# Rotating the start of the gated values inside their tiles

## The chip, the core and the metric

The kernel runs on one core of one Trainium2 chip. The metric is the time of the program on the device in microseconds (us). The program is run several times, and the median counts.

## What is computed

For each batch and head a matrix state of 48 x 48 complex numbers is carried along 768 time steps, decayed by a complex factor and fed with an outer product; its real part is read with q. The result, as a 3072 x 384 matrix, goes through a gated feed-forward block.

```python
batch, n_heads, seq, head_dim = 4, 8, 768, 48          # d_model 384, d_ff 1536
for t in range(S):
    S_re, S_im = ar * S_re - ai * S_im + kv, ar * S_im + ai * S_re
    y[:, :, t] = einsum('bhd,bhde->bhe', q[:, :, t], S_re)
...
g = x @ w_gate
silu = g * (1.0 / (1.0 + np.exp(-g)))
val = x @ w_val
return (silu * val @ w_out).astype(np.float32)
```

## The kernel before

The 3072 tokens are cut into 24 slabs of 128 tokens (four batches times six pieces of 128 steps), and two slabs make a group, so there are 12 groups. The attention part of a group is prepared by VectorE, ScalarE and small matmuls (`stage_ops`, `slab_ops`) and ends in the transposed activations of the group, 256 tokens wide, as a rounded high part `xh` and the rest `xl`. Then the feed-forward part of the group runs (`ffn_ops`), in 12 chunks of 128 of the 1536 inner columns.

For chunk f of group g (g from 1 on; group 0 runs in plain float32 with other tiles) the steps are these. `f1` (line 886) makes the gate and the value of the chunk in one PSUM bank: 18 matmuls, each with its own weight load of 128 x 128 from the weight tiles `ww`, with 256 columns of `xh` or `xl` streaming. ScalarE applies silu into `sg` (line 896), and VectorE multiplies by the value (line 901). The product is split: `hh` is a cast of `sg` to the float32r type (lines 332 on ScalarE or 334 on VectorE, by `cast`), and `hl` is the difference `sg - hh` (line 328, by `tt`). `f2` (line 925) multiplies back: six matmuls, where `hh` or `hl` is the stationary operand (a weight load of 128 x 128 each) and 384 columns of the output weights `wo` stream; for each half of the tokens the order is `hh` with the high weights, `hh` with the low weights, `hl` with the high weights. Twelve chunks accumulate in two PSUM banks, which are then copied to `ost` and stored.

`hh` and `hl` have two buffers each (`slots`), so chunk n waits for what chunk n - 2 left. The order of all instructions on all engines is computed beforehand by a planner that simulates the engines with given costs (`Planner.plan`); f2 of a chunk stands behind f1 of the next chunk or the one after it. The attention work of later groups is put between the chunks of earlier ones.

Tiles are made by `new`. Pools give addresses in the order in which names are first made, and some small tiles stand only to move what follows. In the kernel before, taken modulo 512 bytes, `wo` and the stage tiles begin at 320, `ww` at 384 (tiles 0 to 6 and 9 to 11) or 128 (7, 8 and -1), the values inside `xh` and `xl` at 320 or 64 (`begin` is 48 elements, 192 bytes, into tiles at 128 or 384), the triangular mask at 384, and all buffers of `hh` and `hl` at 128. Slices of a tile that line 886 or 925 uses lie whole multiples of 512 bytes apart. So in f1 and f2 from group 1 on, the stationary operand begins 64 or 320 bytes after the moving one, modulo 512. `hh` and `hl` are the last tiles in the memory.

Of the kernel before, what the change touches and what calls it, by code (L numbers as in the profile page):

```python
# [20 lines left out]
P = 128  # L21
# [4 lines left out]
NF = DF // P  # L26
# [173 lines left out]
def quick(ctx, tc, q, k, v, a_re, a_im, w_in, w_out, out, count):  # L200
# [4 lines left out]
    work = ctx.enter_context(tc.tile_pool(name="work", bufs=1))  # L205
# [66 lines left out]
    for t in STAGES:  # L272
        SHAPE[t] = ([P, 2 * H, D], F32)
    slots = dict(qs=1, ks=1, T=2, dec=3, sc=2, sg=2, hh=2, hl=2, ost=2, xh=2, xl=2, vt=2,
                 gv=2, po=1, ps=2, py=1, pm=1)
# [6 lines left out]
    for t, (nm, f, i) in {"re": ("w", 0, 0), "im": ("w", 0, 1), "s1": ("o", 0, 0), "s2": ("w", 1, 0), "s3": ("w", 1, 1),  # L282
                          "qt": ("o", 1, 0), "kt": ("o", 2, 0), "qs": ("w", 2, 0)}.items():
        n, nm_f = 96 if t == "qs" else D, (nm, NF - 3 + f)
# [12 lines left out]
    def new(tag, inst):  # L297
        if tag in fixed:
            t = fixed[tag][0]
        elif tag[0] in ("ww", "wo", "bt"):  # L300
            t = None
        elif tag == "ps":
            t = banks[int(inst[-1])]
        elif tag in PSUMS:
            t = psum.tile([P, 512], F32, name="p_" + tag, tag=tag, bufs=2 if tag == "po" else slots[tag])
        else:
            shape, dt = SHAPE[tag]
            if isinstance(inst, tuple) and inst[0] in SPLIT:
                dt = F32R
            if tag == "xh" and inst == 0:  # L310
                dt = F32
            if tag == "xl" and isinstance(inst, str):
                dt = U32
            if tag in SHIFTED:
                n = shape[-1] * (shape[1] if len(shape) > 2 else 1)
                begin = 48 if tag[0] == "x" else 0
                t = work.tile([P, n + (64 if begin else 0)], dt, name=tag, tag=tag, bufs=slots[tag])[:, begin:begin + n]
                if len(shape) > 2:
                    t = t.rearrange("p (k t) -> p k t", k=KT)
            elif tag == "dec":  # L320
                t = work.tile([96, 8 * H], dt, name=tag, tag=tag, bufs=slots[tag])[:, 0:4 * H]
            else:
                t = work.tile(shape, dt, name=tag, tag=tag, bufs=slots[tag])
        at_[tag, inst] = t
        return t
# [26 lines left out]
    def stage_ops(g, first, many):  # L352
# [19 lines left out]
        def load(t, x):  # L372
            def fn(e):
                b0 = 2 * bp + first
                nc.sync.dma_start(out=new(*tg(t)).rearrange("p (b h) d -> p b (h d)", b=many), in_=x[b0:b0 + many, :, c * P:c * P + P, :].rearrange("b h t d -> t b (h d)"))  # L375
            pl.add(f"ld_{t}{N}", {"SP": 0.5}, fn, deps=[held.get(t, "")], alloc=[tg(t)], lat=1.4 if N == "0a" and t in ("re", "im") else LAND if exact else LAND + SPARE, move=0.65 * many)

        def act(name, dst, source, func, table, deps, scale=1.0, bias=None, new_=False):
            def fn(e):
                if new_:  # L380
                    new(*tg(dst))
                kw = {} if bias is None else {"bias": bias}
                nc.scalar.activation(out=of(dst), in_=of(source), func=func, scale=scale, **kw)  # L383
            length = cost(("ACT",), span)
            if bias is not None:
                length["ACT"] += 0.1
            pl.add(name + N, length, fn, deps=[d if "." in d else d + N for d in deps] + [held.get(name, "")], alloc=[tg(dst)] if new_ else [],
                   use=[tg(source)] + ([] if new_ else [tg(dst)]), table=table)
# [4 lines left out]
        if divided:  # L393
            def rec(e):
                nc.vector.reciprocal(out=new(*tg("s3")), in_=of("re"))
            pl.add("rec" + N, {"DVE": 2.5 * span / HD}, rec, deps=["ld_re" + N], alloc=[tg("s3")], use=[tg("re")])
        else:
            act("lnr", "s3", "re", AF.Ln, "ln", ["ld_re"], new_=True)
# [815 lines left out]
```

## Time and profile before

| | us |
|---|---|
| median of 3 runs | 611.21 |
| lowest and highest of them | 610.23, 611.64 |
| span of the profiled execution, first to last instruction | 609.42 |
| TensorE multiplying (PE) | 591.6 |
| TensorE loading weights (PEld) | 562.3 |
| VectorE (DVE) busy | 473.0 |
| ScalarE (ACT) busy | 442.3 |
| GpSimd (POOL) busy | 39.3 |

The time of the profiled execution is given only as its span. The weight load of the next matmul runs beside the matmul before it, so PE and PEld overlap. A matmul's busy time reaches beyond the start of the next one, since they are pipelined; the pace of TensorE is read from start to start.

### The profile page before, as it was taken

The numbers are of one execution on the slowest core, as the hardware profiler recorded it, in microseconds if no ns is written. First come the engines' busy times: TensorE is split into PE (matmuls) and PEld (weight loads), VectorE is DVE, ScalarE is ACT, GpSimd is POOL, SyncE is SP. The second block draws the span as 40 slices with busy tenths as digits, with TensorE's granted clock in tenths as the row PEclk, the third lists the DMA queues.
The fourth block names the chain that finished last, engine by engine and source line by source line (L and its number), as shares of the span: only waits on it lengthen the run. The fifth ranks groups of instructions, "written<-read, shape, count | busy, mean of one in ns | idle before, by whom it ended". The sixth has DMA issues, their size and how long they took to land.

```text
span 609.4 us, 18043 instructions
## 1 busy us (share of the span) xinstructions
PE 591.6 (97%) x7516; PEld 562.3 (92%) x7516; DVE 473.0 (78%) x848; ACT 442.3 (73%) x718; POOL 39.3 (6%) x70
## 2 busy tenths in 40 slices
PE   8789999999999999999999999999999999999996
PEld 7577768999999999999999999999999999999996
DVE  8999999889799778678678678678878867553443
ACT  7999898676976977976985994995996896212221
POOL 4210001010010010010010001001000000000000
PEclk9999999999999999999999999999999999999999
DMA  9999114554554465455545445545644642632220
GB/s 278 359 361 348 23 55 112 130 145 106 150 152 102 123 154 130 122 144 134 129 116 149 122 109 148 131 114 125 157 117 116 172 115 65 147 78 58 79 53 31
DMA packets 132263, 83.15 MB, mean 136 GB/s; under 512 B 106416, under 2 KB 123824, under 8 KB 132176
## 3 DMA queue, kind: packets, MB, share of 16 engines
q1 hardware_dynamic: 129344, 77.09, 46.6%
q0 software_dynamic: 2256, 4.06, 2.9%
q8 instruction: 61, 1.00, 0.7%
q10 hardware_dynamic: 576, 0.79, 0.4%
q14 instruction: 26, 0.21, 0.1%
HBM read 61.40 MB, written 4.78 MB: 109 GB/s over the span
## 4 chain that ended last, share of the span: by engine, by line
PE 84%; DVE 4%; DMA 4%; SPq 3%; ACT 3%; issue 2%
PE p_gv L886 46%; PE p_po L925 24%; PE p_py L707 6%; PE p_ps L664 4%; PE p_pm L478 2%; PE p_pm L713 2%; DMA wo<-in_w_out_dram 1%; SPq L785 1%; SPq L375 1%; DMA ww<-in_w_in_dram 1%; DVE ww L328 1%; DMA qt<-in_q_dram 1%; ACT L1031 1%; ACT xl L332 0%; ACT s L383 0%
## 5 line engine op out<-in xcount | busy, mean ns | idle before, releaser
L886 PE MATMUL p_gv<-xh,ww 128*128 128x256 f32 x1596 | 304.0, 288 | 0.0
L886 PEld LDWEIGHTS p_gv<-xh,ww 128*128 128x128 f32 x1596 | 256.0, 189 | 7.3 <-issue 1.4
L886 PE MATMUL p_gv<-xl,ww 128*128 128x256 f32 x726 | 200.9, 277 | 0.7 <-issue 0.7
L1031 ACT ACT_TABLE_LOAD x124 | 159.1, 1283 | 2.3
L886 PEld LDWEIGHTS p_gv<-xl,ww 128*128 128x128 f32 x726 | 136.4, 188 | 0.2 <-issue 0.2
L925 PE MATMUL p_po<-wo,hh 128*128 128x384 f32 x484 | 124.0, 337 | 0.0
L901 DVE TENSOR_TENSOR sg<-sg,p_gv 128x256 f32<-128x256 f32 x144 | 59.0, 411 | 70.4 <-ACT sg L896 67.2
L896 ACT ACTIVATE sg<-p_gv 128x256 f32<-128x256 f32 x144 | 54.3, 383 | 75.1 <-PE p_gv L886 74.5
L925 PEld LDWEIGHTS p_po<-wo,hh 128*128 128x128 f32 x484 | 81.6, 188 | 0.9 <-issue 0.2
L925 PE MATMUL p_po<-wo,hl 128*128 128x384 f32 x242 | 81.0, 336 | 0.0
L328 DVE TENSOR_TENSOR hl<-sg,hh 128x256 fp32r<-128x256 f32 x132 | 54.7, 421 | 8.0 <-ACT hh L332 2.3
L332 ACT CAST hh<-sg 128x256 fp32r<-128x256 f32 x74 | 30.1, 407 | 30.2 <-DVE sg L901 25.1
L925 PEld LDWEIGHTS p_po<-wo,hl 128*128 128x128 f32 x242 | 45.4, 188 | 0.0
L383 ACT ACTIVATE s<-s 128x768 f32<-128x768 f32 x44 | 37.2, 845 | 10.9 <-DVE s L328 9.2
L707 PE MATMUL p_py<-sc,vt 128*32 128x128 f32 x768 | 37.3, 272 | 2.4 <-ACT ww-1_529 L332 2.4
L664 PEld LDWEIGHTS p_ps<-T 96*32 96x32 f32 x1536 | 28.9, 111 | 4.8 <-issue 3.4
L707 PE MATMUL p_py<-T,G 96*32 96x128 f32 x640 | 33.2, 274 | 0.0
L678 DVE TENSOR_TENSOR sc<-p_ps,tri 128x512 f32<-128x512 f32 x48 | 31.1, 678 | 2.2 <-PE p_py L707 2.2
L664 PE MATMUL p_ps<-T 96*32 96x128 f32 (+3 forms) x1536 | 32.2, 235 | 0.0
L328 DVE TENSOR_TENSOR ks<-kt,s 128x768 f32<-128x768 f32 x22 | 20.9, 952 | 8.3 <-PE p_pm L713 6.7
L707 PEld LDWEIGHTS p_py<-sc,vt 128*32 128x32 f32 x768 | 23.3, 110 | 3.4 <-issue 3.0
L328 DVE TENSOR_TENSOR qs<-qt,s 128x768 f32<-128x768 f32 x22 | 20.8, 950 | 5.1 <-ACT s L383 5.1
(147 smaller groups left out, 839.6 us busy)
## 6 DMA issues: line engine op xcount, KB each, us to landing
T<-turned SPq DMA_DIRECT2D x240, 64.0 KB, 2.1
wo<-in_w_in_dram SPq DMA_DIRECT2D x24, 384.0 KB, 3.6
ww<-in_w_in_dram SPq DMA_DIRECT2D x12, 767.8 KB, 10.5
vt<-in_v_dram SPq DMA_DIRECT2D x24, 288.0 KB, 4.0
wo<-in_w_out_dram SPq DMA_DIRECT2D x12, 384.0 KB, 3.2
wo<-in_w_out_dram SPq DMA_DIRECT2D x12, 383.8 KB, 10.9
re<-in_a_re_dram SPq DMA_DIRECT2D x11, 384.0 KB, 3.8
im<-in_a_im_dram SPq DMA_DIRECT2D x11, 384.0 KB, 4.5
```

What stands on the lines that cost most here:

```text
L328: V[e].tensor_tensor(out=out, in0=a, in1=b, op=op)
L332: nc.scalar.copy(out=out, in_=in_)
L383: nc.scalar.activation(out=of(dst), in_=of(source), func=func, scale=scale, **kw)
L478: nc.tensor.matmul(out=ps, lhsT=tri, rhs=flat(half(x, i)), start=j == 0, stop=j == 1)
L664: nc.tensor.matmul(out=ps[32 * slot:32 * slot + 32, at, 32 * j:P], lhsT=kT[:, h // 2, h % 2, j, :], rhs=qT[:, h // 2, h % 2, j:4, :], star ...
L678: nc.vector.tensor_tensor(out=s.rearrange("p (x h) t -> p x h t", x=2), in0=at_["ps", f"{n}.{qd}"].rearrange("p (x h t) -> p x h t", x=2, ...
L707: nc.tensor.matmul(out=o, lhsT=l, rhs=r, start=opens, stop=closes, tile_position=(0, 32 * slot))
L886: nc.tensor.matmul(out=gv[:, i, :], lhsT=l, rhs=r, start=(m == 0), stop=(m == len(mm) - 1))
L896: nc.scalar.activation(out=new("sg", I), in_=at_["gv", I][:, 0:2 * P], func=AF.Silu)
L901: nc.vector.tensor_tensor(out=sg, in0=sg, in1=at_["gv", I][:, 2 * P:4 * P], op=ALU.mult)
L925: nc.tensor.matmul(out=po, lhsT=l[:, cs], rhs=weight("o", f, part), start=f == 0 and j == 0, stop=f == NF - 1 and j == len(products) - 1)
L1031: nc.scalar.preload_act_table_set(op.load)
```

## The change

In `new`, the values of `hh` and `hl` no longer begin where their buffer begins. Their instance is named "g.f", and from it a start of 4 * (11 * (12 * (g - 1) + f) % 32) elements of four bytes is computed: a multiple of 16 bytes from 0 to 496. Each buffer has 128 elements (512 bytes) more room. `xh` and `xl` keep their start of 48 elements. The same view is written by the cast and the subtraction and read by line 328 and by the weight loads of line 925.

```diff
             if tag in SHIFTED:
                 n = shape[-1] * (shape[1] if len(shape) > 2 else 1)
-                begin = 48 if tag[0] == "x" else 0
-                t = work.tile([P, n + (64 if begin else 0)], dt, name=tag, tag=tag, bufs=slots[tag])[:, begin:begin + n]
+                if tag[0] == "x":
+                    begin, room = 48, 64
+                else:
+                    g, f = map(int, inst.split("."))
+                    begin, room = 4 * (11 * (NF * (g - 1) + f) % 32), 128
+                t = work.tile([P, n + room], dt, name=tag, tag=tag, bufs=slots[tag])[:, begin:begin + n]
```

## Rows read from the trace of the kernel before

**Rows 1.** Page, part 1: busy us (share of the span) x instructions, by engine.

```profile
PE 591.6 (97%) x7516; PEld 562.3 (92%) x7516; DVE 473.0 (78%) x848; ACT 442.3 (73%) x718; POOL 39.3 (6%) x70
```

**Rows 2.** Page, part 4: the chain that ended last, by line.

```profile
PE p_gv L886 46%; PE p_po L925 24%; PE p_py L707 6%; PE p_ps L664 4%; PE p_pm L478 2%; PE p_pm L713 2%; DMA wo<-in_w_out_dram 1%; SPq L785 1%; SPq L375 1%; DMA ww<-in_w_in_dram 1%; DVE ww L328 1%; DMA qt<-in_q_dram 1%; ACT L1031 1%; ACT xl L332 0%; ACT s L383 0%
```

**Rows 3.** By windows: length, busy PE, PEld, DVE, ACT, POOL, granted clock, DMA, GB/s.

```profile
324.00:353.20 29.20, 28.51 (x362) 27.93 (x361) 22.09 (x39) 23.62 (x37) 0.58 (x1) 1.00 0.50 130
353.20:602.00 248.80, 247.69 (x3136) 242.92 (x3130) 167.81 (x327) 150.60 (x271) 6.75 (x11) 1.00 0.43 108
```

**Rows 4.** Timeline of PE, one regular chunk: start us, busy us, instruction, xcount merged.

```profile
585.10 0.51 PE L925 MATMUL p_po<-wo,hh 128*128 128x384 f32 x2
585.44 0.34 PE L925 MATMUL p_po<-wo,hl 128*128 128x384 f32 x1
...
586.13 0.28 PE L886 MATMUL p_gv<-xh,ww 128*128 128x256 f32 x1
...
588.18 0.51 PE L925 MATMUL p_po<-wo,hh 128*128 128x384 f32 x2
```

**Rows 5.** Timeline of PE from 332.5 to 349.2: f2 starts, and one f1.

```profile
332.79 0.52 PE L925 MATMUL p_po<-wo,hh 128*128 128x384 f32 x2
...
339.15 0.52 PE L925 MATMUL p_po<-wo,hh 128*128 128x384 f32 x2
...
340.21 0.28 PE L886 MATMUL p_gv<-xh,ww 128*128 128x256 f32 x1
...
342.33 0.52 PE L925 MATMUL p_po<-wo-1_589,hh 128*128 128x384 f32 x2
...
348.69 0.52 PE L925 MATMUL p_po<-wo,hh 128*128 128x384 f32 x2
```

**Rows 6.** Timeline of PE at 325.2: an f1 matmul after a stop.

```profile
325.20 0.28 PE L886 MATMUL p_gv<-xl,ww 128*128 128x256 f32 x1 [0.69 <-issue]
```

**Rows 7.** Tile `hh`: operation xcount, ns min/median/max, first and last start, shapes.

```profile
L925 PEld LDWEIGHTS p_po<-wo,hh x484: 186/188/192, 110.8 to 603.2; 128*128 128x128 f32 x162
...
L328 DVE TENSOR_TENSOR hl<-sg,hh x132: 407/420/428, 106.8 to 602.6; 128x256 fp32r<-128x256 f32 x132
L332 ACT CAST hh<-sg x74: 386/407/419, 114.9 to 589.3; 128x256 fp32r<-128x256 f32 x74
L334 DVE CAST hh<-sg x58: 278/294/297, 105.8 to 602.3; 128x256 fp32r<-128x256 f32 x58
```

**Rows 8.** Timeline of all engines from 598.4 to 604.2: the last two chunks.

```profile
598.96 0.43 DVE L328 TENSOR_TENSOR hl<-sg,hh 128x256 fp32r<-128x256 f32 x1
...
601.54 0.51 PE L925 MATMUL p_po<-wo,hh 128*128 128x384 f32 x2
...
602.26 0.29 DVE L334 CAST hh<-sg 128x256 fp32r<-128x256 f32 x1
...
602.59 0.42 DVE L328 TENSOR_TENSOR hl<-sg,hh 128x256 fp32r<-128x256 f32 x1
...
602.79 0.96 PE L925 MATMUL p_po<-wo,hh 128*128 128x384 f32 x4
...
603.59 0.51 PE L925 MATMUL p_po<-wo,hl 128*128 128x384 f32 x2
```

**Rows 9.** Page, part 5: groups; xcount | busy us, mean ns of one | idle before.

```profile
L886 PE MATMUL p_gv<-xl,ww 128*128 128x256 f32 x726 | 200.9, 277 | 0.7 <-issue 0.7
...
L925 PE MATMUL p_po<-wo,hh 128*128 128x384 f32 x484 | 124.0, 337 | 0.0
...
L925 PE MATMUL p_po<-wo,hl 128*128 128x384 f32 x242 | 81.0, 336 | 0.0
```

**Rows 10.** Groups by line, the smaller ones: as in the group before.

```profile
L886 PE MATMUL p_gv<-xl,ww-1_529 128*128 128x256 f32 x66 | 18.3, 277 | 0.0
...
L925 PE MATMUL p_po<-wo-1_589,hh 128*128 128x384 f32 x44 | 11.2, 335 | 0.0
...
L925 PE MATMUL p_po<-wo-1_589,hl 128*128 128x384 f32 x22 | 7.4, 336 | 0.0
```

## The prediction

> **What bounds the kernel now.** I read the page's busy times first, then its chain of waits, then the table by windows, then the groups by line, and last the timeline of TensorE, which the argument rests on. TensorE multiplies during 591.6 of 609.4 us, its weight loads cover 562.3, and VectorE and ScalarE stand at 78% and 73% [rows 1]. In the chain that ended last, line 886 (the first matmuls, "f1") has 46% and line 925 (the second, "f2") 24%; no line that writes the gated values `hh` and `hl` is named among the largest [rows 2]. From 353 to 602 us TensorE is busy for 247.7 of 248.8 us, at a granted clock of 1.00, the 2.4 GHz level [rows 3]. So only a change of TensorE's own pace can move the end by much, or a late `hh` or `hl`.
>
> That pace shows in the distance from start to start (the busy time of one matmul overlaps the next one's). In a regular chunk the six f2 matmuls take 586.13 - 585.10 = 1.03 us and the eighteen f1 matmuls 588.18 - 586.13 = 2.05, in all 3.08 [rows 4]. The same instructions run slower in one stretch: f2 340.21 - 339.15 = 1.06, f1 342.33 - 340.21 = 2.12, in all 3.18; six chunks begin 3.18 us apart, from 332.79 to 348.69 [rows 5]. The clock in that stretch is granted at 1.00 as well [rows 3], so this is not the clock. The stretch opens after TensorE had stood still for 0.69 us at 325.20 [rows 6]. I read this as two paces in which the stream of the moving operand and the weight load beside it can settle, about 4 ns a matmul apart, and I call them fast and slow. I count 7 slow chunks: these six and the rest of that stretch.
>
> **The change part by part.** It adds and removes no instruction, wait or DMA, and gives the planner the same costs, so the order stays. It moves where each chunk's `hh` and `hl` begin, in steps of 16 bytes. Per chunk k = 12(g-1)+f the step is 11k mod 32, so that the 132 chunks visit each of 32 starts four or five times.
>
> *The tiles.* Each of the four slots grows by 512 bytes; they lie last, so no other tile moves. 0 us.
>
> *The writes.* Per chunk there is one cast into `hh` (74 on ScalarE of 386 to 419 ns, 58 on VectorE of 278 to 297) and one subtraction into `hl` (407 to 428) [rows 7]. At their fixed starts the spread is 11 to 33 ns. No row shows another start. From above: a VectorE cast could fall to the subtraction's median, 420 - 294 = 126 ns more, 58 x 0.126 = 7.3 us of VectorE's time. From below: nothing gained, since what they finish early waits anyway. Cover: the subtraction that ends at 598.96 + 0.43 = 599.39 serves the f2 at 601.54, 2.1 us later [rows 8]. Without cover stands only the last chunk: its cast at 602.26 releases the f2 at 602.79, while its `hl` (done at 603.01) is wanted at 603.59 [rows 8]. So 0 to 0.13 us; I take 0.
>
> *The weight loads and the f2 matmuls.* These read the moved values: 792 matmuls (484 + 44 on `hh`, 242 + 22 on `hl`) [rows 9, 10], each with its own weight load, which in the groups takes 186 to 192 ns [rows 7] and runs beside the matmul before it. Before the change every such pair stands alike: the weights begin 64 or 320 bytes past the moving operand, modulo 512. That 64 or 320 makes no difference is to be seen: 277 ns for the low values against the common weight tiles, 277 against the one whose start is 256 bytes off (`ww-1`) [rows 9, 10]. What 16, 32 or 128 bytes do, no row shows. The bounds come from the two paces. From above: all chunks slow, (132 - 7) x 0.10 = 12.5 us. From below: the first two matmuls of f2 take 585.44 - 585.10 = 0.34 [rows 4]; six at 0.17 make 1.02 instead of 1.03, 132 x 0.01 = 1.3 us gained; and if nothing but columns counted, 384 at 2.4 GHz are 0.160, six 0.96, a gain of 132 x 0.07 = 9.2 us, as an estimate that no matmul of these rows reaches.
>
> My value lies between: a start 16 bytes on is, to the weight load, the same as reading at another moment beside the stream, and such another moment is what parts slow from fast. With nothing known of 31 of 32 starts, I take half of the chunks as slow in f2: (66 - 7) x 0.03 = 1.8 us. f1 reads nothing that moved, but in the slow stretch the pace was handed from f2 to the f1 behind it and back through six chunks [rows 5]. I take it as handed on in half of these cases, a quarter of all: (33 - 7) x 0.07 = 1.8 us. Sum: 1.8 + 1.8 = 3.6 us. The profiled span of 609.4 becomes 613.0; no time of that execution besides its span is given, and the span lies 1.8 under the median of the three runs, 611.21. So 611.2 + 3.6 = 614.8 us.
>
> One rule speaks against this term. The Trainium skill, "TensorE: Matmul & The Clock Gate", section "Step-by-step: what each phase is for", says that TensorE has two independent read ports, one for the moving operand and one for weights, so that loading the next weights takes nothing from the running matmul. By it the sum is 0 and the time 611.2. The rows agree only in part: by the same page's section "Back-to-back issue gap" 256 columns would take 262 cycles, 109 ns, and f1 takes 2.05 / 18 = 114 in the fast pace and 2.12 / 18 = 118 in the slow one [rows 4, 5].
>
> **The rivals.**
>
> *No start matters (611.2).* The two streams do not touch. For it: 64 and 320 bytes cost the same, and the weight load keeps to 186 to 192 ns through both paces [rows 7, 10]. Against it: something other than work and clock sets two paces, and it has to do with how the two reads stand to each other. The remaining difference is that of runs, 610.2 to 611.6. If it holds, the slow pace is a matter of timing after stops alone, and the starts of `hh` do not choose it.
>
> *Most starts are bad (about 621).* f2 goes slow at nearly every start, and f1 keeps the pace as it did for six chunks: with 107 of 132 slow, (107 - 7) x 0.10 = 10 us, 621. For it: nothing in the stretch from 332.79 to 348.69 brought the pace back [rows 5]. Against it: for most of the run the fast pace returns after each stop, and f1's own pairs stay as they were.
>
> *The other side: faster (609.1).* The present start of `hh` against `wo` is a poor one, and f2's 1.03 is partly lost time; other starts give 0.17 per matmul and a start that changes with every chunk leaves the slow pace no room to last. Then 132 x 0.01 + 7 x 0.10 = 2.0 us are gained. Place: the 792 f2 matmuls and the stretch of [rows 5]. It decides once more than half of the starts run under 1.03 and none tips f1. For it: f2's 0.172 per matmul stands 12 ns above its columns, f1's 0.114 only 7 above its own. Against it: f1's steps scaled from 256 to 384 columns give 0.171 already, so little is left at this level.
>
> **How the numbers follow.** Forecast 0.47, no effect 0.28, most starts bad 0.11, faster 0.14. What can be told from no change is about 0.2%, 1.2 us. The range runs from 609.7, which leaves out most of the faster case (0.09), to 622, which leaves out the far end of the bad case and a third pace that no row shows (0.09). Since cases of both signs are in it: the forecast's own range is 612.2 to 619. Slower by over 0.2%: 0.43 of the forecast, 0.11, and 0.03 of the no-effect case, 0.57. Same: the rest of the forecast, 0.04, most of no effect, 0.22, and 0.02 of faster, 0.28. Faster: 0.12 and 0.03, 0.15.
>
> **What would show it.** Right: f2's six matmuls take between 1.02 and 1.06 us by chunk, and the value repeats with the step (k and k + 32 alike, perhaps k + 16); slow chunks are several times 7, and f1 takes 2.12 behind some slow f2; line 925's matmuls become longer on average, and VectorE's and ScalarE's casts keep their 294 and 407 ns. Wrong: f2 stays at 1.03 for all starts (no effect); f2 moves with the step but f1 never follows, which halves the sum; f2 falls under 1.03 for most steps; or a third pace far above 1.06, which would carry the time over the range. A wait of line 925 for `hh` or `hl` that is longer than before would say that the writes count after all.

## The result and the profile after

The changed kernel takes 615.45 us (615.02 to 615.88, 4 runs) against 611.42 before (610.23 to 612.5, 4 runs). The ratio is 1.0073, with a 95% interval of 1.0052 to 1.0094; here and below the ratio is estimated from the runs with its interval and is not exactly the quotient of the two medians. The forecast was 614.8, slower.

The order of the work is the same; the change's four added lines move line 886 to 890, 925 to 929, 328 to 332, 332 to 336 and 334 to 338. First the busy times and the groups by line of the changed kernel, which answer to [rows 1] and [rows 9].

```profile
PE 595.0 (97%) x7516; PEld 565.9 (92%) x7516; DVE 472.7 (77%) x848; ACT 442.6 (72%) x718; POOL 39.4 (6%) x70
...
L890 PE MATMUL p_gv<-xl,ww 128*128 128x256 f32 x726 | 201.9, 278 | 0.0
...
L929 PE MATMUL p_po<-wo,hh 128*128 128x384 f32 x484 | 125.2, 340 | 0.0
...
L929 PE MATMUL p_po<-wo,hl 128*128 128x384 f32 x242 | 81.4, 337 | 0.0
```

TensorE multiplies for 3.4 us longer, while VectorE and ScalarE stay within 0.3. The f2 matmuls on `hh` went from 337 to 340 ns. f1, which reads nothing that moved, is longer too. Next the tile `hh`, which answers to [rows 7].

```profile
L929 PEld LDWEIGHTS p_po<-wo,hh x484: 186/188/192, 111.2 to 606.8; 128*128 128x128 f32 x162
...
L332 DVE TENSOR_TENSOR hl<-sg,hh x132: 406/420/427, 107.4 to 606.1; 128x256 fp32r<-128x256 f32 x132
L336 ACT CAST hh<-sg x74: 386/407/419, 115.4 to 592.6; 128x256 fp32r<-128x256 f32 x74
L338 DVE CAST hh<-sg x58: 274/294/297, 106.4 to 605.8; 128x256 fp32r<-128x256 f32 x58
```

All medians are those of before: neither the writes nor the recorded weight loads depend on the start. The loss is in the distance from one matmul to the next. The timeline of TensorE over two chunks of the changed kernel, the first of step 16 (256 bytes), the second of step 27:

```profile
545.61 0.51 PE L929 MATMUL p_po<-wo,hh 128*128 128x384 f32 x2
...
546.65 0.28 PE L890 MATMUL p_gv<-xh,ww 128*128 128x256 f32 x1
...
548.69 0.51 PE L929 MATMUL p_po<-wo,hh 128*128 128x384 f32 x2
...
549.75 0.28 PE L890 MATMUL p_gv<-xh,ww 128*128 128x256 f32 x1
...
551.87 0.34 PE L929 MATMUL p_po<-wo,hh 128*128 128x384 f32 x1
```

The first has the fast pace of [rows 4]: f2 1.04, f1 2.04, in all 3.08. The second has that of [rows 5]: 1.06, 2.12, 3.18. Both stand inside a stretch of 247 us at a granted clock of 1.00 (table by windows, columns as in [rows 3]):

```profile
353.00:600.00 247.00, 245.91 (x3153) 241.19 (x3152) 166.82 (x319) 151.44 (x272) 6.75 (x11) 1.00 0.42 109
```

The pace goes with the step. Chunk 49 of the changed kernel (step 27) began its f2 at 299.33:

```profile
299.33 0.51 PE L929 MATMUL p_po<-wo,hh 128*128 128x384 f32 x2
...
300.39 0.28 PE L890 MATMUL p_gv<-xh,ww 128*128 128x256 f32 x1
...
302.51 0.51 PE L929 MATMUL p_po<-wo,hh 128*128 128x384 f32 x2
```

It takes 1.06 and 2.12 like the one at 548.69, chunk 113. Chunk 33 (from 239.73 to 242.91), at step 11 and so 256 bytes away from these, takes 3.18 as well. I took all chunks whose f2 and f1 run without a stop between them and summed the distances from start to start, by step modulo 16 (f is the number of the chunk in its group, 0 to 11):

| step mod 16 | f2, us | f1 behind it, us |
|---|---|---|
| 0 | 1.036 to 1.040; 1.052 in chunk 0 | 2.043 to 2.044; 2.058 in chunk 0 |
| 6, 9, 10, 12 | 1.044 to 1.059 | 2.118 to 2.125 |
| 11 | 1.057 to 1.058; 1.040 for f = 5, behind attention matmuls | 2.119; 2.053 to 2.054 for f = 5 |
| the ten others | 1.039 to 1.064 | 2.044 to 2.063 |

Step 0 alone gives both best values; what precedes the chunk counts too. Since each step of the rotation stands 11 after the one before, a step always follows the same other one, so the table does not part a step's own price from what the chunk before it leaves. Behind 19 of 87 f2 that are followed by an uninterrupted f1, this f1 takes over 2.09; before the change it was 6 of 87. In sums over both traces from the first f2 to the last, the 748 f2 distances without a stop grew from 129.5 to 131.2 us, 1.6 in all. The 2322 f1 distances with their stops grew from 269.1 to 270.4, 1.3: a pace slower by 1.2 ns a matmul, 2.6 us, less 1.3 by which the stops were longer before. Of these 1.3, 0.9 are the stop of [rows 6], which this execution does not have. The remaining 1.0 of the 4.0 us between the spans lies almost all outside these chunks: 0.5 ahead of the first f2, whose first weight load begins at 108.1 instead of 107.6, and 0.4 behind the last f2; no moved value is read there.

### The profile page after: what moved, and what is told of

Same layout as the page of the kernel before. It is cut to its first block, busy times and chain, and to the rows that moved or that the text cites. A ratio compares the mean times of both kernels' runs of the same rounds, so it can differ in the third digit from the quotient of the medians.

```text
span 613.4 us, 18043 instructions
## 1 busy us (share of the span) xinstructions
PE 595.0 (97%) x7516; PEld 565.9 (92%) x7516; DVE 472.7 (77%) x848; ACT 442.6 (72%) x718; POOL 39.4 (6%) x70
## 4 chain that ended last, share of the span: by engine, by line
PE 84%; DVE 5%; DMA 3%; ACT 2%; SPq 2%; issue 2%
PE p_gv L890 46%; PE p_po L929 24%; PE p_py L711 6%; PE p_ps L668 4%; PE p_pm L482 2%; PE p_pm L717 2%; DMA wo<-in_w_out_dram 1%; SPq L789 1%; DVE ww L332 1%; DMA ww<-in_w_in_dram 1%; SPq L379 1%; DMA ww<-in_a_im_dram 1%; ACT L1035 1%; DVE ww L796 1%; ACT xl L336 0%
## 5 line engine op out<-in xcount | busy, mean ns | idle before, releaser
L668 PE MATMUL p_ps<-T 96*32 96x32 f32 (+3 forms) x1536 | 32.2, 235 | 0.0
L890 PE MATMUL p_gv<-xh,ww-1_529 128*128 128x256 f32 x132 | 24.8, 280 | 0.0
```

What stands on the lines that cost most here:

```text
L668: nc.tensor.matmul(out=ps[32 * slot:32 * slot + 32, at, 32 * j:P], lhsT=kT[:, h // 2, h % 2, j, :], rhs=qT[:, h // 2, h % 2, j:4, :], star ...
L890: nc.tensor.matmul(out=gv[:, i, :], lhsT=l, rhs=r, start=(m == 0), stop=(m == len(mm) - 1))
```

## The experiments

All kernels issue the same instructions in the same order. Where a diff shows only a line with `begin, room`, it stands in the place of that line in the change's diff; the others are against the kernel before. In the traces below, line 925 or 929 opens f2 and line 886 or 890 opens f1.

**One fixed start, 160 bytes, for all chunks.**

```diff
-                    begin, room = 4 * (11 * (NF * (g - 1) + f) % 32), 128
+                    begin, room = 40, 128
```

> Every chunk's hh and hl begin 160 bytes into their buffers (step 10); the start no longer changes from chunk to chunk. Theory P (the place of the weight load against the moving operand, modulo 256 bytes, sets each chunk's pace): every chunk is like the chunks of step 10 under the rotation, f2 1.055 and f1 2.12 us instead of 1.036 and 2.044, so 132 x 0.096 = 12.7, less the 0.7 that slow chunks of the kernel before cost already: 623 to 624 us. Rival R (a start that changes redraws the pace, the place itself does not matter): no change from chunk to chunk, so 611.4.

Measured: 615.2 us against 610.9, ratio 1.0061 (1.0038 to 1.0084). Both expectations missed. The start does not change and yet the kernel is slower, so R falls; but the loss is a third of what P gave. The timeline of TensorE, two chunks, f2 and f1 starts:

```profile
288.08 0.52 PE L929 MATMUL p_po<-wo,hh 128*128 128x384 f32 x2
...
289.14 0.28 PE L890 MATMUL p_gv<-xh,ww-1_529 128*128 128x256 f32 x1
...
291.26 0.51 PE L929 MATMUL p_po<-wo,hh 128*128 128x384 f32 x2
...
292.30 0.28 PE L890 MATMUL p_gv<-xh,ww 128*128 128x256 f32 x1
...
294.34 0.34 PE L929 MATMUL p_po<-wo,hh 128*128 128x384 f32 x1
```

Slow and fast chunks take turns: f2 1.06 and f1 2.12, then 1.04 and 2.04. A chunk entered at the fast pace leaves slow, and one entered slow leaves fast. The two buffers of `hh` and `hl` take turns as well, but they do not decide. Chunk 18, counted from 0 over all groups and so an even one, is entered from an f1 of 2.05; it takes 1.05 (from 177.44 to 178.49), and the f1 after it, behind two attention matmuls, 2.12 (178.84 to 180.96). The even chunk 46, at 291.26 above, takes 1.04 and 2.04. So the start and the pace in which the chunk is entered decide together; that second part was missing in P.

**Start at 0 or 256 bytes, changed every second chunk.**

```diff
+                    begin, room = 64 * ((NF * (g - 1) + f) // 2 % 2), 128
```

> The start changes every second chunk between 0 and 256 bytes. Theory P: 256 bytes on is the same place, so 611.4 within 0.2%, f2 1.036 and f1 2.044 in every regular chunk. Rival R: the pace is redrawn at each change of start, half of 132 chunks, so some 2 us and more: 613 to 615. A period of 512 bytes instead of 256: half of the chunks at another pace than 1.036, the time anywhere from 611 to 618.

Measured: 611.5 against 610.9, ratio 1.0011 (0.9994 to 1.0027). The timeline across a change of start:

```profile
577.83 0.51 PE L929 MATMUL p_po<-wo,hh 128*128 128x384 f32 x2
...
580.91 0.51 PE L929 MATMUL p_po<-wo,hh 128*128 128x384 f32 x2
...
583.99 0.51 PE L929 MATMUL p_po<-wo,hh 128*128 128x384 f32 x2
...
587.07 0.33 PE L929 MATMUL p_po<-wo,hh 128*128 128x384 f32 x1
```

The first two chunks begin at 256 bytes, the third, at 583.99, at 0: 3.08 each. A change of start by itself costs nothing, and 256 bytes on is the same place. 128 bytes on is not: step 8 gave 1.044 and 2.057 in the rotated kernel, where step 0, entered from the same f1 time of 2.061, gave 1.036 and 2.044.

**Everything 160 bytes further on.**

```diff
-    const.tile([P, 32], F32, name="before_tri")
+    const.tile([P, 72], F32, name="before_tri")
```

> All tiles of the kernel, hh, hl, wo, ww, xh, xl and the masks, lie 160 bytes further on; every distance between two of them stays as in the kernel before. Theory P (relative place): 611.4. Rival A (the absolute place of the stationary operand decides; hh and hl now begin where step 10 puts them): 623 to 624 as with 160 bytes for hh and hl alone, f2 1.055 and f1 2.12.

Measured: 611.0 against 610.9, ratio 0.9991 (0.9973 to 1.001). The timeline of one chunk:

```profile
568.12 0.51 PE L925 MATMUL p_po<-wo,hh 128*128 128x384 f32 x2
...
569.15 0.28 PE L886 MATMUL p_gv<-xh,ww 128*128 128x256 f32 x1
...
571.20 0.33 PE L925 MATMUL p_po<-wo-1_589,hh 128*128 128x384 f32 x1
```

1.03, 2.05, 3.08, as in [rows 4]. `hh` and `hl` begin at the same offset modulo 512 bytes as in the first experiment, where they were alone in moving. So distances between tiles count, and where the values lie in the memory does not.

**One chunk in twelve at 160 bytes.**

```diff
+                    begin, room = 40 if f == 9 else 0, 128
```

> Only chunk f = 9 of each group begins at 160 bytes, the other eleven at 0. Chunk 9 opens a stretch of about six chunks with nothing but f1 and f2. Theory H (the pace is handed on, as the prediction assumed): f2 of chunk 9 tips the stretch, and chunks 10, 11, 0, 1, 2 stay slow behind it, 11 groups x 6 x 0.096 = 6.3: about 617.5. Theory O (each chunk's own start alone sets its f2 and the f1 behind it): 11 x 0.096 = 1.1: about 612.5.

Measured: 612.3 against 610.9, ratio 1.0016 (1.0002 to 1.0029). By the time H falls, and O's size holds. A usual stretch:

```profile
287.86 0.52 PE L929 MATMUL p_po<-wo,hh 128*128 128x384 f32 x2
...
288.92 0.28 PE L890 MATMUL p_gv<-xh,ww-1_529 128*128 128x256 f32 x1
...
291.04 0.51 PE L929 MATMUL p_po<-wo,hh 128*128 128x384 f32 x2
...
292.07 0.28 PE L890 MATMUL p_gv<-xh,ww 128*128 128x256 f32 x1
...
294.12 0.51 PE L929 MATMUL p_po<-wo,hh 128*128 128x384 f32 x2
```

Chunk 9 costs 3.18, and the next one, at 0 bytes, is back at 3.08. So it goes in nine of the eleven groups. In two another kind of stretch stands, as in [rows 5]:

```profile
383.64 0.51 PE L929 MATMUL p_po<-wo,hh 128*128 128x384 f32 x2
...
386.82 0.52 PE L929 MATMUL p_po<-wo,hh 128*128 128x384 f32 x2
...
390.00 0.52 PE L929 MATMUL p_po<-wo,hh 128*128 128x384 f32 x2
```

Here chunk 10, at 0 bytes, takes 3.18 too, and so do the next two. The displaced chunk 9, at 383.64, did not open this stretch: the f1 ahead of chunk 8 is slow already, 16 matmuls from 375.82 to 377.70, 118 ns each. So at the usual start there are at least two slow settings with the same f1 time. One ends with the next f2. The other goes on through many chunks; here and in [rows 5] it also outlived the attention matmuls between chunks 8 and 9, and it ended with those between chunks 2 and 3 of the next group. A displaced f2 leads into the first; the second is that of the kernel before, and what leads into it was not settled. The trace is of an execution of 616.1 us, 3.8 above the median: its first f2 begins at 110.21, 2.4 us later than in the trace of the kernel before, and the two stretches cost about 1 us.

**Only `hl`, and only `hh`, at 160 bytes.**

```diff
+                    begin, room = 40 if tag == "hl" else 0, 128      # the other run: "hh"
```

> hl alone begins at 160 bytes, hh at 0: 264 of the 792 weight loads stand at another place. Theory L (the load and the matmul beside it lose the time): the loads of hl run beside the second and the fifth matmul of f2, so in a chunk entered at the fast pace these two grow, the others stay: with both tiles at 160 the six were 176, 178, 175, 180, 174, 172 ns instead of 170, 173, 173, 174, 173, 173, so 170, 178, 173, 174, 174, 173, f2 1.042 us and 0.8 us in all at most, f1 2.044: 611.0 to 612. Rival S (any shift of phase in f2 tips the f1 behind it): every second f1 at 2.12 as with both tiles, 66 x 0.077 = 5 us: about 615.

> hh alone begins at 160 bytes, hl at 0: 528 of 792 loads. Theory L: the first, third and fourth matmul of f2 grow (176, 173, 175, 180, 173, 173), f2 1.050, 132 x 0.014 = 1.8 us, and f1 keeps its 2.044 because the last load of hl stands as before: 612.5 to 613. Rival S: every second f1 at 2.12, 5 us more: about 615 to 617.

Measured: `hl` alone 611.2 against 611.7, ratio 1.0000 (0.9984 to 1.0015); `hh` alone 613.7, ratio 1.0046 (1.0026 to 1.0066). A chunk with `hl` moved:

```profile
572.07 0.50 PE L929 MATMUL p_po<-wo-1_589,hh 128*128 128x384 f32 x2
...
573.11 0.28 PE L890 MATMUL p_gv<-xh,ww 128*128 128x256 f32 x1
...
575.15 0.33 PE L929 MATMUL p_po<-wo,hh 128*128 128x384 f32 x1
```

And one with `hh` moved:

```profile
574.20 0.51 PE L929 MATMUL p_po<-wo-1_589,hh 128*128 128x384 f32 x2
...
575.25 0.28 PE L890 MATMUL p_gv<-xh,ww 128*128 128x256 f32 x1
...
577.31 0.51 PE L929 MATMUL p_po<-wo,hh 128*128 128x384 f32 x2
```

With `hl` f2 is 1.04 and f1 2.04; from start to start the six are 170, 172, 177, 176, 175, 173 ns, 1.043. With `hh` f2 is 1.05 and f1 2.06; the six are 176, 173, 180, 174, 172, 178 ns, 1.053. L holds for the sizes of f2 (1.042 and 1.050 expected) and for f1 with `hl`. S falls in both: no f1 takes over 2.09 with `hl`, and 7 of 87 do with `hh`. L misses which matmul pays: with `hl` the third and fourth grow most, where the second and fifth were expected; with `hh` the first, third and sixth, where the first, third and fourth were. And f1 behind a moved `hh` is slower by 0.017, which L did not have; the time of 613.7 is above L's 612.5 to 613 and under S's 615 to 617.

**All chunks at 16 bytes.**

```diff
+                    begin, room = 4, 128
```

> All chunks begin at 16 bytes (step 1), which under the rotation gave f2 1.063 and f1 2.044. If the place alone decides, every regular chunk repeats these: 132 x 0.027 = 3.6 at most, about 614, with f1 at the fast pace throughout. If the pace in which the chunk is entered decides as well, as with 160 bytes where 1.055 and 1.040 took turns, f2 is 1.063 only behind another step, and both numbers change.

Measured: 616.5 against 611.7, ratio 1.0080 (1.0055 to 1.0105). Within the intervals, sixteen bytes in all chunks cost as much as the rotation. The timeline:

```profile
288.32 0.51 PE L929 MATMUL p_po<-wo,hh 128*128 128x384 f32 x2
...
289.37 0.28 PE L890 MATMUL p_gv<-xh,ww-1_529 128*128 128x256 f32 x1
...
291.49 0.51 PE L929 MATMUL p_po<-wo,hh 128*128 128x384 f32 x2
...
292.54 0.28 PE L890 MATMUL p_gv<-xh,ww 128*128 128x256 f32 x1
...
294.59 0.51 PE L929 MATMUL p_po<-wo,hh 128*128 128x384 f32 x2
```

f1 is 2.12 and 2.05 in turns. The same step gave f1 2.044 in the rotated kernel, behind another step. So the second of the two cases expected holds.

**`wo` moved along with `hh` and `hl`.**

```diff
-    work.tile([P, 48], F32, name="ahead", tag="ahead", bufs=1)
+    work.tile([P, 88], F32, name="ahead", tag="ahead", bufs=1)
...
-    work.tile([P, 16], F32, name="behind", tag="behind", bufs=1)
+    work.tile([P, 104], F32, name="behind", tag="behind", bufs=1)
...
+                    begin, room = 40, 128
```

> hh and hl begin at 160 bytes in all chunks, and wo (with the stage tiles that lie behind it) is moved by 160 bytes too, while ww, xh, xl and the mask stay. Against wo, hh and hl stand as in the kernel before; the first load of hh against xh, and that of ww beside the sixth f2 matmul against wo, do not. Theory P: f2's first five matmuls return to 170 to 174 ns; what is lost is at the borders, f2 1.036 to 1.045. Rival (the place against xh, or where hh is written, decides): f2 keeps 1.055 and 1.040 in turns, and f1 2.12 every second time, 615 as with hh and hl alone.

Measured: 615.0 against 611.7, ratio 1.0048 (1.003 to 1.0066).

```profile
287.40 0.52 PE L929 MATMUL p_po<-wo,hh 128*128 128x384 f32 x2
...
288.45 0.28 PE L890 MATMUL p_gv<-xh,ww-1_529 128*128 128x256 f32 x1
...
290.57 0.51 PE L929 MATMUL p_po<-wo,hh 128*128 128x384 f32 x2
...
291.61 0.28 PE L890 MATMUL p_gv<-xh,ww 128*128 128x256 f32 x1
...
293.65 0.34 PE L929 MATMUL p_po<-wo,hh 128*128 128x384 f32 x1
```

Mixed. f2 falls to 1.047 and 1.039 in turns, nearer to P, whose upper bound was 1.045. But f1 still takes 2.12 every second time, as the rival had it, and the time is the rival's 615, though the six loads stand right against `wo` again, all but the border ones: the first of `hh` beside `xh` and that of `ww` beside `wo`. This fits two border loads being enough to tip f1; it does not show which of them.

**`xh` and `xl` moved instead.**

```diff
-                begin = 48 if tag[0] == "x" else 0
-                t = work.tile([P, n + (64 if begin else 0)], dt, name=tag, tag=tag, bufs=slots[tag])[:, begin:begin + n]
+                begin = 88 if tag[0] == "x" else 0
+                t = work.tile([P, n + (128 if begin else 0)], dt, name=tag, tag=tag, bufs=slots[tag])[:, begin:begin + n]
```

> hh and hl stay; instead the values of xh and xl begin 160 bytes further on, so that in f1 the moving operand is the one that is displaced (18 of 24 matmuls of a chunk), and in f2 nothing but the first load of hh. Theory P (what counts is the place of the two reads against each other, whichever is moved): f1 loses as f2 did, between 2.044 and some 2.12 us or a third pace above, f2 nearly as before: 132 x 0.05 to 0.08 = 6 to 10 us, 617 to 622. Rival F (only the 384-column matmuls of f2 are touchy, f1 merely follows): f1 stays at 2.044, the time at 611 to 612.

Measured: 625.9 against 611.0, ratio 1.0249 (1.0219 to 1.028).

```profile
583.28 0.51 PE L925 MATMUL p_po<-wo,hh 128*128 128x384 f32 x2
...
584.32 0.28 PE L886 MATMUL p_gv<-xh,ww 128*128 128x256 f32 x1
...
586.48 0.34 PE L925 MATMUL p_po<-wo-1_589,hh 128*128 128x384 f32 x1
```

f1 takes 2.16, a third pace, and a chunk 3.20. F falls: f1 is touched just as f2 is, and moving the streaming side does it too. The size, 14.9 us, was above the expected 6 to 10, and f2 did not stay nearly as before: it takes 1.046 to 1.065 over the trace instead of 1.036, though only its first load was displaced. The larger room for `xh` and `xl` moves what lies behind them by whole multiples of 256 bytes, which the run with starts of 0 and 256 shows to be the same place for `hh` and `hl`.

None of these versions is faster than the kernel before.

## Why the prediction was right

*The bound.* It held: TensorE's pace alone moved the end. The writes cost nothing, as taken; the last chunk's too.

*The term of f2, 1.8 us.* Measured 1.6. The picture behind it was too simple: f2 does not have two values, of which half the starts get the slow one. Fifteen of sixteen places cost something in this order of steps, mostly 7 to 28 ns a chunk. That their mean came near half of the slow pace's 0.03 is luck.

*The term of f1, 1.8 us.* Measured 2.6 in pace, so this term was too small. I took a quarter of the chunks as slow behind f2; it was 19 of 87. But the other 68 take 2.052 on average instead of 2.044, which the prediction had at nothing: of 1.56 us by which the 87 grew, 1.0 comes from 13 more f1 at 2.12 and the rest from these small rises. The reason given, that f2 hands its pace on, is half right: a displaced f2 does set the f1 behind it, but at the usual start the next f2 ends it. The stretch of [rows 5], on which this step rested, is another setting.

*The sum, 3.6 us.* The medians differ by 4.0. In the traces the pace grew by 4.3, the stops gave back 1.3, and 1.0 came from outside the chunks. So the mechanism and the direction were right, and that the sum came within 0.4 us is in part luck. Two figures of the prediction are off without entering the sum: the spreads of [rows 7] are 19 to 33 ns, not 11 to 33, and 2.0 us gained would have given 609.2, not 609.1.

*"64 or 320 makes no difference."* Right, and extended by the run with starts of 0 and 256 bytes.

*The rule that spoke against it.* The Trainium skill, "TensorE: Matmul & The Clock Gate", section "Step-by-step: what each phase is for", has the loading of the next weights take no SBUF read bandwidth from the running matmul, since each has its own read port. By that no start should matter. The measurements differ: with the same instructions in the same order, 16 bytes between the two reads cost 0.8%, and 160 bytes on the side of `xh` 2.5%. Here the measurement decides; whether bandwidth or something else in the two reads is lost, no run shows. The 262 cycles of the Trainium skill's section "Back-to-back issue gap" are for a matmul by itself, while f1 runs in pairs of load and matmul, so 114 and 118 ns speak neither for the rule nor against it.

*The rivals.* No effect: out, the interval excludes 1. Most starts bad: f2 yes, but not at that price, since f1 follows only some of them. Faster: out; no place of the sixteen gave an f2 under 1.036.

What is shown: the cost hangs on the distance between the stationary and the moving operand, modulo 256 bytes for `hh` and `hl`, and on what the chunk before leaves. What stays open: what in the reads collides, which matmul pays for which load, which border load tips f1, and what opens and ends the long slow stretches. In the kernel before all pairs stand at 64 bytes modulo 256; no run gave all pairs another common distance, so it is not shown that 64 is the best.

## What to carry to other kernels

When TensorE is busy without gaps, compare its distances from start to start with those of the same instructions elsewhere in the trace: 4 ns on an f1 matmul of 114 are 3.5% of its pace, and neither the waits nor the busy share of TensorE (97% before and after) show them. Treat the distance between the starts of the stationary and the moving operand as a parameter to be measured (here modulo 256 bytes, in steps of 16), and keep it the same for all pairs that follow each other, as the kernel before does; whoever pads or moves one tile changes it for its partners. Changes that alter no instruction cost between 0.5% (`hh` alone) and 2.5% (`xh` and `xl`) here.

## What the runs showed of the hardware

A run of the same matmuls can have several paces that repeat, at one granted clock (1.00 from 110 to 600 us in the changed kernel and in those with 160 bytes for `hh` and `hl` or for `xh` and `xl`): 2.04, 2.06, 2.12 and 2.16 us for the eighteen of f1. With one fixed start two of them can alternate from chunk to chunk (1.04 + 2.04 and 1.06 + 2.12 at 160 bytes). I had not expected that a tile's start matters through what the chunk before it left behind, nor that moving the streamed tile of f1 by 160 bytes costs 14.9 us.
